# Products with kv and key sums as two matmuls of 64 stationary columns each, and second-layer weight loads placed by due time alone

## The chip, the cores and the metric

The kernel runs on one core of a Trainium2 chip. The metric is the device time of one execution in microseconds (us); less is better. TensorE (PE in the profile) multiplies matrices: it loads a stationary operand of up to 128 columns (PEld, the weight load), streams a moving operand past it and adds into PSUM. VectorE (DVE) and ScalarE (ACT) do everything elementwise, SyncE (SP) issues the DMAs. Each engine works through its own queue in order and waits for the others by semaphores. TensorE's clock is granted at one of two levels, 1.2 or 2.4 GHz; the profile gives it as a share of the upper one.

## The reference, cut to what matters

Linear attention with random features, then two feed-forward layers on its output:

```python
def phi(x):
    proj = np.einsum('bhsd,md->bhsm', x, omega)
    h = proj - np.sum(x * x, axis=-1, keepdims=True) / 2.0
    h = h - np.max(h, axis=-1, keepdims=True)
    return np.exp(h) / np.sqrt(m)
q_p, k_p = phi(q * scale), phi(k * scale)
kv = np.einsum('bhsm,bhsd->bhmd', k_p, v)           # key sums, 128 features x 64 per head
z = np.sum(k_p, axis=2)
num = np.einsum('bhsm,bhmd->bhsd', q_p, kv)         # products with kv
den = np.einsum('bhsm,bhm->bhs', q_p, z)[..., None] + 1e-06
x = (num / den)                                     # 4 batches x 576 tokens, 8 heads x 64
...
h = x @ w_in;  x = softplus(h) @ w_out              # layer 1: 512 -> 2048 -> 512
h = x @ w_in2; x = silu(h) @ w_out2                 # layer 2, the same sizes
```

There are 4 batches, 8 heads, 576 tokens a batch, 64 elements a head and 128 features. The layers' weights come as float64 and are turned into pairs of float32 parts on the core.

## The kernel before

**The attention.** The tokens are cut into 8 tiles of 256 (two a batch, n = 0 to 7) and one tile of the 256 tokens that are left (n = 8, 64 of each batch). `k_half` handles four heads of a key tile: two projections (`pp_k`), row maxima on DVE, the exponential on ACT (`phi`), and then the key sums `pkv_k` at L489: for each of the two pairs of heads (e = 0, 1) four products of float32, stationary operand a 128x128 tile of phi, moving operand 64 columns of v and a column of ones, so 65. The result is added to the batch's sums `kv` on DVE. `q_half` does the same for queries, and then transposes phi on TensorE (`pq`, L541), copies it back on ACT (`qt`, L545), multiplies it with `kv` (`pn`, L553: again four products of 128 stationary and 65 moving columns for each e), divides by the last column on DVE (`den`, `xn`, L564 to L567), and transposes the quotient on TensorE (`px`, L575), from which ACT and DVE make the layer's input `x`. A product of float32 shows as two passes in the trace, each a weight load and a matmul. The query tile n = 8 mixes four batches; its products at L557 already have 64 stationary columns, two beside each other: one for the first 64 tokens of the tile, written to PSUM partitions 0 to 63, the other for the second 64 tokens, to partitions 64 to 127.

**The layers.** The 2304 tokens go through as five blocks (sb = 0 to 3 of 512, sb = 4 of 256). In a block each of 16 chunks (fc) of the 2048 inner columns takes 12 matmuls `h` (L633 to L635; three products of high and low parts for each of four slices), then ACT and DVE make `g` and its two parts `ghl`, then 12 matmuls `y` (L656 in layer 1, L664 in layer 2). I write H(layer, sb, fc) and Y(layer, sb, fc) for these groups of 12. The attention of batch b + 1 runs between the groups of block (0, b); the attention of batch 0 comes ahead of all.

**Weights.** `weights(layer, fc, io, after)` loads 512 KB of float64 (`raw`, L278) and makes the two float32 parts from them: on ACT L284 and L301, on DVE L288, L292, L296 and the difference at L209. A raw tile sits in one of 4 buffers of tag `b4`, the finished weights in one of 16 of tag `wt`. The second layer's weights take over the buffers of the first layer's, and are made during block (0, 4) and block (1, 0).

**What sets the order.** Nothing of this is ordered by hand. Every step is given to `Order` (L53) with its engine, a planned cost, what it depends on, the buffers that it takes, and a due time. `due1` (L247 to L254) holds the planned time at which each H starts; steps get due times by counting back from it. `run` (L93) then simulates four engines and takes, for the engine that can start earliest, the step with the least due time among those that could start within 0.05 us of each other. `after` is the earliest planned time of a load. So each number in the cost table (L41 to L50) and each `after` can move any instruction on any engine. The layers' weights, `x`, and the attention share DVE, ACT and SP.

Of the kernel before, what the change touches and what calls it, by code (L numbers as in the profile page):

```python
# [28 lines left out]
NT = NB - 1  # L29
# [8 lines left out]

G1, G2, G3 = 0.2267, 0.117, 0.224  # L41
V5, V2, VS = (0.60, 0.15), (0.33, 0.15), (0.15, 0.15)
VF, VA, VH = (0.33, 0.15), (0.20, 0.15), (0.35, 0.15)
A5, A2, AE, AL, AX2 = (0.52, 0.17), (0.30, 0.15), (1.0, 0.2), (0.97, 0.17), (1.02, 0.2)
# [146 lines left out]
def attention_moe_moe_kernel(  # L191
# [15 lines left out]
    def diff(o, a, b):  # L207

        nc.vector.tensor_tensor(o, a, b, op=ALU.subtract)  # L209

    E = mybir.EngineType
    ctx.enter_context(tc.manual_schedule(engines={E.SP, E.Activation, E.DVE, E.PE}))
    const = ctx.enter_context(tc.tile_pool(name="const", bufs=1))
# [34 lines left out]
    for layer in range(2):  # L248
        for sb in range(NSB):
            full = width[sb] == 2 * T  # L250
            for fc in range(NFC):
                due1[layer, sb, fc] = t
                t += (24 * G1 if full else 12 * (G2 + (G1 / 2 if layer else G2))) + ((1.9 if sb else 2.2) if layer == 0 and sb < B else 0)
    due1["end"] = t  # L254

    def bits_pair():
# [214 lines left out]
    def k_half(n, half, simple, psums, due, after):  # L471
        s = {}
        name = f"k{n}_{half}"
        hs = slice(4 * half, 4 * half + 4)
        ins = inputs(s, name, kT[n, :, 2 * half : 2 * half + 2, :], kN[n, :, :, hs, :], [(v1[n, :, :, hs, :], (2, 4))], simple, simple, after)
        cols, sq_of = main_cols()
        phis = features(s, name, simple, ins, cols, sq_of, psums)
        tk = new(psums())
        b, h0 = n // 2, 4 * half
        both = []  # L480
        for e, (x, tphi) in enumerate(phis):

            def kv(e=e):
                phi, v = s["phi", e], s["v", 0]
                if "pkv" not in s:
                    s["pkv"] = get(tk["tag"], [P, 4, D + 1], F32, f"pkv_{name}")
                for j in range(2):
                    for c in range(2):
                        nc.tensor.matmul(  # L489
                            s["pkv"][:, 2 * e + j], phi[:, 2 * c + j, :], v[:, c, 2 * e + j, :], start=(c == 0), stop=(c == 1)  # L490
                        )

            both.append(add("PE", 4 * G3, kv, [x, ins[4][0]] + both, alloc=[] if e else [tk], uses=[tphi, ins[5][0]] + ([tk] if e else [])))
        chain(b, h0, add("DVE", VH, lambda: kv_add(b, h0, s["pkv"]), both, due=due, uses=[tk]))

    def k_tail(bp, simple, psums, due, after):
# [25 lines left out]
    def q_half(n, half, simple, psums, due, after):  # L522
# [12 lines left out]
        for e, (x, tphi) in enumerate(phis):  # L535
# [11 lines left out]
            def num(e=e, tn=tn):  # L547
                pn = s["pn", e] = get(tn["tag"], [P, 4, D + 1], F32, f"pn_{name}_{e}")
                qt = s["qt", e]
                for i in range(4):  # L550
                    h = 4 * half + 2 * e + i % 2
                    if n < NT:
                        nc.tensor.matmul(pn[:, i, :], qt[:, i, :], kvs[n // 2][:, h, :], start=True, stop=True)  # L553
                    else:
                        for a in range(2):
                            rs = slice(a * TAIL, (a + 1) * TAIL)
                            nc.tensor.matmul(  # L557
                                pn[rs, i, :], qt[:, i, rs], kvs[2 * (i // 2) + a][:, h, :], start=True, stop=True
                            )
# [23 lines left out]
                sums = [i for b in range(B) for i in kv_last[b, half]]  # L583
            f1 = add("PE", 0.45, flip, [x], alloc=[tq], uses=[tphi])
            c1 = add("ACT", A5, copy, [f1], alloc=[tqs], uses=[tq])
            n1 = add("PE", (4 if n < NT else 8) * G3, num, [c1] + sums, alloc=[tn], uses=[tqs])
            o1 = add("DVE", (0.5, 0.2), norm, [n1], alloc=[td, txn], uses=[tn])
            backs.append(add("PE", 0.23, back, [o1] + backs, alloc=[] if e else [tx], uses=[txn] + ([tx] if e else [])))

# [184 lines left out]
    for sb in range(NSB):  # L774
        if sb + 1 < NSB:
            attention(sb + 1, late_banks)
        if sb == NSB - 1:
            for fc in range(NFC):
                for io in range(2):
                    weights(1, fc, io, due1[0, NSB - 1, 0] + 2.8 * fc + 2.0)  # L780
        block(0, sb)
    for sb in range(NSB):
        x2(sb, due1[1, sb, 0] - 25.0)
# [66 lines left out]
```

## Time and profile before

| what | value |
|---|---|
| three runs, median | 972.95 us (972.69 to 976.61) |
| the profiled execution | 972.0 us, of it 970.2 us span from the first to the last instruction |
| PE matmuls | 943.5 us busy, 97% of the span, 4936 passes |
| PE weight loads | 803.3 us busy, 83% |
| DVE | 427.6 us busy, 44% |
| ACT | 443.3 us busy, 46% |
| mean granted TensorE clock | 0.994 |
| L553, `pn` with 128 stationary columns | 256 passes, 31.2 us busy, mean 275 ns |
| L489, `pkv` | 128 passes with v in `x_k` (16.2 us) and 128 with v in `v_k` (16.0 us) |
| L557, `pn` with 64 stationary columns | 64 passes, 2.3 us busy |

How to read it: matmuls are pipelined, so the busy time of a row of matmuls is the union of overlapping spans, and the duration of one (275 ns) is its way through the array, not the time that it keeps the next one waiting. What a matmul costs in a stream is the distance from its start to the next one's. Shares over the whole span hide that DVE and ACT are nearly full in the first fifth and mostly idle later.

### The profile page before, as it was taken

Reading aid. Unit: us, or ns where it says so; the run is one execution under the profiler, and the core shown is the slowest. Engines: PE = TensorE matmul, PEld = TensorE weight load, DVE = VectorE, ACT = ScalarE, POOL = GpSimd, SP = SyncE. Lnnn points to the kernel's source line nnn. Section 1 sums busy time; section 2 is a strip of 40 time slices with the busy share of each in tenths; the row PEclk is TensorE's granted clock in tenths of the full one; section 3 lists DMA queues with packets and bytes.
Section 4 is the critical chain, followed back from the end, with each engine's and each line's share of the span. In section 5 each row is a group of like instructions: output and inputs, shape, how many; then the busy total and the mean of one; then the engine's idle time right before and its main releaser. Section 6 shows DMA issues by size and latency. Waiting matters only on the chain.

```text
span 970.2 us, 12523 instructions
## 1 busy us (share of the span) xinstructions
PE 943.5 (97%) x4936; PEld 803.3 (83%) x4936; DVE 427.6 (44%) x923; ACT 443.3 (46%) x810; POOL 1.2 (0%) x7
## 2 busy tenths in 40 slices
PE   8899999999999999999999999999999999999994
PEld 7678778888888888887889988888888888888893
DVE  6987889455535453442112999521111112111210
ACT  7888878555555555442213776332222122221220
POOL 0000000000000000000000000000000000000000
PEclk9999999999999999999999999999999999999998
DMA  9643443222012221010003666202002000100100
GB/s 332 217 141 131 154 151 109 87 88 77 22 34 77 78 65 33 1 45 1 0 1 131 217 197 217 75 12 76 0 9 79 1 1 11 60 1 6 44 1 22
DMA packets 38159, 72.86 MB, mean 75 GB/s; under 512 B 3412, under 2 KB 18388, under 8 KB 38100
## 3 DMA queue, kind: packets, MB, share of 16 engines
q1 hardware_dynamic: 37970, 71.79, 22.0%
q8 instruction: 39, 0.64, 0.3%
q10 hardware_dynamic: 130, 0.26, 0.1%
q14 instruction: 20, 0.16, 0.1%
HBM read 62.60 MB, written 9.44 MB: 74 GB/s over the span
## 4 chain that ended last, share of the span: by engine, by line
PE 86%; DVE 5%; ACT 5%; DMA 2%; issue 1%; SPq 0%; ACTq 0%; DVEq 0%
PE y L664 20%; PE y L656 18%; PE h L633 13%; PE h L635 13%; PE h L634 13%; PE pkv_k L489 2%; PE pn_q L553 2%; PE pq_q L541 1%; DMA xN_q<-in_qN 1%; ACT phi_k L429 1%; DVE wt L209 1%; DVE wf L292 1%; ACT L641 1%; ACT L429 1%; PE px_q L575 1%
## 5 line engine op out<-in xcount | busy, mean ns | idle before, releaser
L209 DVE TENSOR_TENSOR ghl<-g,ghl 128x512 fp32r<-128x512 f32 (+1 forms) x160 | 101.9, 637 | 413.1 <-ACT ghl L642 411.6
L641 ACT ACTIVATE g<-h 128x512 f32<-128x512 f32 (+1 forms) x160 | 88.6, 554 | 333.4 <-PE h L635 332.9
L633 PE MATMUL h<-x,wt 128*128 128x512 f32 (+1 forms) x640 | 238.2, 372 | 0.4 <-ACT ghl L642 0.4
L634 PE MATMUL h<-x,wt 128*128 128x512 f32 (+1 forms) x640 | 235.8, 368 | 0.9 <-DVE x L209 0.9
L635 PE MATMUL h<-x,wt 128*128 128x512 f32 (+1 forms) x640 | 236.0, 369 | 0.0
L656 PE MATMUL y<-ghl,wt 128*128 128x512 f32 (+1 forms) x960 | 213.8, 372 | 0.0
L664 PE MATMUL y<-wt,ghl 128*128 128x512 f32 x864 | 208.6, 390 | 0.0
L656 PEld LDWEIGHTS y<-ghl,wt 128*128 128x128 f32 x960 | 166.2, 189 | 28.4
L664 PEld LDWEIGHTS y<-wt,ghl 128*128 128x128 f32 x864 | 161.3, 188 | 32.8
L634 PEld LDWEIGHTS h<-x,wt 128*128 128x128 f32 x640 | 120.8, 189 | 21.0 <-DVE x L209 1.3
L633 PEld LDWEIGHTS h<-x,wt 128*128 128x128 f32 x640 | 120.7, 189 | 20.4 <-ACT ghl L642 0.8
L635 PEld LDWEIGHTS h<-x,wt 128*128 128x128 f32 x640 | 120.7, 189 | 20.4
L642 ACT ACTIVATE ghl<-h 128x512 fp32r<-128x512 f32 (+1 forms) x160 | 88.1, 550 | 35.7 <-PE y L664 29.3
L284 ACT ACTIVATE wf<-raw 128x512 f32<-128x512 f32 x64 | 43.1, 681 | 13.8 <-DVE wt L209 13.5
L301 ACT CAST wt<-wf 128x512 fp32r<-128x512 f32 x64 | 39.4, 624 | 16.4 <-DVE wf L296 15.9
L209 DVE TENSOR_TENSOR wt<-wf,wt 128x512 fp32r<-128x512 f32 x64 | 43.2, 685 | 5.3 <-ACT wt L301 5.2
L292 DVE SCALAR_TENSOR_TENSOR wf<-wf,raw 128x512 uint32<-128x512 uint32 x64 | 43.0, 685 | 1.5 <-ACT wf L284 1.1
L296 DVE SCALAR_TENSOR_TENSOR wf<-raw,wf 128x512 uint32<-128x512 uint32 x64 | 43.1, 684 | 0.2
L641 ACT ACT_TABLE_LOAD x29 | 37.2, 1283 | 11.8 <-PE h L635 11.5
L409 DVE TENSOR_REDUCE mn_q<-pp_q 128x4 f32<-128x512 f32 x36 | 24.4, 686 | 24.3 <-PE pp_q L405 24.3
L553 PEld LDWEIGHTS pn_q<-kv,qt_q 128*128 128x128 f32 x256 | 30.8, 192 | 5.0 <-ACT qt_q L545 4.1
L553 PE MATMUL pn_q<-kv,qt_q 128*128 128x65 f32 x256 | 31.2, 275 | 2.4 <-ACT qt_q L545 2.4
(103 smaller groups left out, 708.8 us busy)
## 6 DMA issues: line engine op xcount, KB each, us to landing
raw<-in_w SPq DMA_DIRECT2D x64, 512.0 KB, 3.7
out<-y_sb SPq DMA_DIRECT2D x17, 256.0 KB, 2.2
y_dram<-y_sb SPq DMA_DIRECT2D x16, 256.0 KB, 2.0
x2raw<-y_dram SPq DMA_DIRECT2D x16, 256.0 KB, 3.8
xT_q<-in_qT SPq DMA_DIRECT2D x14, 256.0 KB, 2.9
xN_q<-in_qN SPq DMA_DIRECT2D x14, 256.0 KB, 3.1
x_k<-in_v SPq DMA_DIRECT2D x8, 260.0 KB, 5.3
v_k<-in_v SPq DMA_DIRECT2D x8, 260.0 KB, 3.0
```

The costliest lines, as they stand in the source:

```text
L209: nc.vector.tensor_tensor(o, a, b, op=ALU.subtract)
L284: nc.scalar.activation(s["f"], hif, AF.Copy, scale=2.0**-112)
L292: nc.vector.scalar_tensor_tensor(fu, fu, 3, lo, op0=ALU.logical_shift_left, op1=ALU.bitwise_or)
L296: nc.vector.scalar_tensor_tensor(fu, hi, 0x80000000, fu, op0=ALU.bitwise_and, op1=ALU.bitwise_or)
L553: nc.tensor.matmul(pn[:, i, :], qt[:, i, :], kvs[n // 2][:, h, :], start=True, stop=True)
L633: nc.tensor.matmul(ph[:, :w], wt[:, 0, 0, cs], xt[:, 0, cc, :w], start=(cc == 0), stop=False)
L634: nc.tensor.matmul(ph[:, :w], wt[:, 0, 0, cs], xt[:, 1, cc, :w], start=False, stop=False)
L635: nc.tensor.matmul(ph[:, :w], wt[:, 0, 1, cs], xt[:, 0, cc, :w], start=False, stop=(cc == NCC - 1))
L641: nc.scalar.activation(g, s["h"][:, :w], f)
L642: nc.scalar.activation(ghl[:, 0, :w], s["h"][:, :w], f)
L656: nc.tensor.matmul(py[dm][:, :w], wt[:, 1, a, cs], g[:, x, :w], start=(first and i == 0), stop=(last and i == 2),)
L664: nc.tensor.matmul(py[c], g[:, x, cs], wt[:, 1, a, :], start=(first and i == 0), stop=(last and i == 2),)
```

## The change

- `by_halves` replaces each product of `pkv` and of `pn` for n < 8 by two matmuls: columns 0 to 63 of the stationary operand into PSUM partitions 0 to 63, columns 64 to 127 into partitions 64 to 127, both with the same 65 moving columns. There are 128 such products in `pkv` (16 `k_half`, 8 each) and 128 in `pn` (16 `q_half`, 8 each). The tail of the keys (L511) and everything else keep their shapes.
- The planner is told 0.116 us for such a product in place of 0.224 us (G4 for G3), and the same for the products of n = 8 at L557, whose planned total falls from 8 * 0.224 to 4 * 0.116 us for each e.
- The planned allowance for attention in each chunk of blocks (0, 1) to (0, 3) falls from 1.9 to 1.6 us.
- The loads of the second layer's weights lose their earliest planned time.

```diff
-G1, G2, G3 = 0.2267, 0.117, 0.224
+G1, G2, G3, G4 = 0.2267, 0.117, 0.224, 0.116
...
+    def by_halves(o, a, b, **flags):
+
+        for c in range(2):
+            r = slice(c * 64, c * 64 + 64)
+            nc.tensor.matmul(o[r], a[:, r], b, **flags)
...
-                t += (24 * G1 if full else 12 * (G2 + (G1 / 2 if layer else G2))) + ((1.9 if sb else 2.2) if layer == 0 and sb < B else 0)
+                t += (24 * G1 if full else 12 * (G2 + (G1 / 2 if layer else G2))) + ((1.6 if sb else 2.2) if layer == 0 and sb < B else 0)
...
-                        nc.tensor.matmul(
-                            s["pkv"][:, 2 * e + j], phi[:, 2 * c + j, :], v[:, c, 2 * e + j, :], start=(c == 0), stop=(c == 1)
-                        )
-
-            both.append(add("PE", 4 * G3, kv, [x, ins[4][0]] + both, alloc=[] if e else [tk], uses=[tphi, ins[5][0]] + ([tk] if e else [])))
+                        by_halves(s["pkv"][:, 2 * e + j], phi[:, 2 * c + j, :], v[:, c, 2 * e + j, :], start=(c == 0), stop=(c == 1))
+
+            both.append(add("PE", 4 * G4, kv, [x, ins[4][0]] + both, alloc=[] if e else [tk], uses=[tphi, ins[5][0]] + ([tk] if e else [])))
...
-                        nc.tensor.matmul(pn[:, i, :], qt[:, i, :], kvs[n // 2][:, h, :], start=True, stop=True)
+                        by_halves(pn[:, i, :], qt[:, i, :], kvs[n // 2][:, h, :], start=True, stop=True)
...
-            n1 = add("PE", (4 if n < NT else 8) * G3, num, [c1] + sums, alloc=[tn], uses=[tqs])
+            n1 = add("PE", 4 * G4, num, [c1] + sums, alloc=[tn], uses=[tqs])
...
-                    weights(1, fc, io, due1[0, NSB - 1, 0] + 2.8 * fc + 2.0)
+                    weights(1, fc, io, 0.0)
```

Because the planner's numbers change, the order changes nearly everywhere in small ways. `pkv` still stands in runs of four products, each between other matmuls, and `pn` in runs of eight (e = 0 and 1 behind each other). Three places are shown as the built programs have them.

The first is on PE, in block (0, 3): the end of the second half of the query tile n = 8, whose quotient DVE makes before `px` can transpose it. Before:

```order
L557 MATMUL pn_q8_1_1_4179<-kv2_90,qt_q8_1_1_4163 64x65
L557 MATMUL pn_q8_1_1_4179<-kv3_91,qt_q8_1_1_4163 64x65
L575 MATMUL px_q8_1_4193<-ident_74,xn_q8_1_0_4191 128x128 x2
L656 MATMUL y_0_3_0_4049<-ghl_0_3_3_4134,wt_0_3_723 128x512 x3
L656 MATMUL y_0_3_1_4050<-ghl_0_3_3_4134,wt_0_3_723 128x512 x3
L656 MATMUL y_0_3_2_4051<-ghl_0_3_3_4134,wt_0_3_723 128x512 x3
L656 MATMUL y_0_3_3_4052<-ghl_0_3_3_4134,wt_0_3_723 128x512 x3
L575 MATMUL px_q8_1_4193<-ident_74,xn_q8_1_1_4211 128x128 x2
```

and now:

```order
L561 MATMUL pn_q8_1_1_4458<-kv2_90,qt_q8_1_1_4445 64x65
L561 MATMUL pn_q8_1_1_4458<-kv3_91,qt_q8_1_1_4445 64x65
L660 MATMUL y_0_3_0_4353<-ghl_0_3_3_4386,wt_0_3_830 128x512 x3
L660 MATMUL y_0_3_1_4354<-ghl_0_3_3_4386,wt_0_3_830 128x512 x3
L660 MATMUL y_0_3_2_4355<-ghl_0_3_3_4386,wt_0_3_830 128x512 x3
L660 MATMUL y_0_3_3_4356<-ghl_0_3_3_4386,wt_0_3_830 128x512 x3
L579 MATMUL px_q8_1_4491<-ident_74,xn_q8_1_0_4470 128x128 x2
```

The first `px` stood right behind the products and now stands behind the 12 matmuls of Y(0, 3, 3). For the first half of the tile (q8_0) the same happens with H(0, 3, 2).

The second is on PE at the end of block (0, 1), at the last query half of batch 2, q5_1. Before:

```order
L553 MATMUL pn_q5_1_0_2858<-kv2_90,qt_q5_1_0_2839 128x65 x4
L553 MATMUL pn_q5_1_1_2867<-kv2_90,qt_q5_1_1_2856 128x65 x4
L656 MATMUL y_0_1_0_1971<-ghl_0_1_14_2824,wt_0_14_1693 128x512 x3
L656 MATMUL y_0_1_1_1972<-ghl_0_1_14_2824,wt_0_14_1693 128x512 x3
L656 MATMUL y_0_1_2_1973<-ghl_0_1_14_2824,wt_0_14_1693 128x512 x3
L656 MATMUL y_0_1_3_1974<-ghl_0_1_14_2824,wt_0_14_1693 128x512 x3
L575 MATMUL px_q5_1_2895<-ident_74,xn_q5_1_0_2875 128x128 x2
```

and now:

```order
L660 MATMUL y_0_1_0_2106<-ghl_0_1_15_3038,wt_0_15_1910 128x512 x3
L660 MATMUL y_0_1_1_2107<-ghl_0_1_15_3038,wt_0_15_1910 128x512 x3
L660 MATMUL y_0_1_2_2108<-ghl_0_1_15_3038,wt_0_15_1910 128x512 x3
L660 MATMUL y_0_1_3_2109<-ghl_0_1_15_3038,wt_0_15_1910 128x512 x3
L215 MATMUL pn_q5_1_0_3071<-kv2_90,qt_q5_1_0_3053 64x65 x8
L215 MATMUL pn_q5_1_1_3080<-kv2_90,qt_q5_1_1_3069 64x65 x8
L579 MATMUL px_q5_1_3099<-ident_74,xn_q5_1_0_3092 128x128 x2
```

Here `px` moved the other way, to right behind the products that feed it. The same is so in block (0, 0) for q2_1 and q3_0, and there `pn` of q3_1 now follows its transposes `pq` with nothing between them.

The third is on SP, in block (0, 4): the loads of the second layer's weights (raw_1_fc_io) and of its first input (x2raw_0). Before:

```order
L278 DMA raw_1_2_1_4872<-in_w2 128x512
L278 DMA raw_1_4_0_4896<-in_w2 128x512
L278 DMA raw_1_3_1_4952<-in_w2 128x512
L719 DMA x2raw_0_0_4955<-y_dram_73 128x512
L719 DMA x2raw_0_1_4973<-y_dram_73 128x512
L719 DMA x2raw_0_2_4980<-y_dram_73 128x512
L278 DMA raw_1_5_0_4985<-in_w2 128x512
L278 DMA raw_1_4_1_5025<-in_w2 128x512
L278 DMA raw_1_6_0_5042<-in_w2 128x512
L719 DMA x2raw_0_3_5047<-y_dram_73 128x512
```

and now:

```order
L284 DMA raw_1_5_1_5232<-in_w2 128x512
L284 DMA raw_1_7_0_5236<-in_w2 128x512
L284 DMA raw_1_6_1_5294<-in_w2 128x512
L284 DMA raw_1_8_0_5318<-in_w2 128x512
L723 DMA x2raw_0_0_5372<-y_dram_73 128x512
L723 DMA x2raw_0_1_5376<-y_dram_73 128x512
L723 DMA x2raw_0_2_5395<-y_dram_73 128x512
L284 DMA raw_1_7_1_5401<-in_w2 128x512
L284 DMA raw_1_9_0_5406<-in_w2 128x512
L723 DMA x2raw_0_3_5447<-y_dram_73 128x512
```

Six of the weight loads now stand ahead of the stores of block (0, 3), and x2raw_0_0 stands behind 16 weight loads where it stood behind 9.

## Rows read from the trace of the kernel before

**Rows 1.** Busy time by stretch: PE, PEld, DVE, ACT, POOL busy (instructions), PEclk, DMA share, GB/s.

```profile
30.00:142.00 112.00, 104.55 (x562) 87.30 (x561) 93.39 (x222) 93.07 (x189) 0.00 (x0) 0.98 0.45 148
142.00:424.00 282.00, 282.00 (x1555) 243.56 (x1554) 148.26 (x344) 157.98 (x228) 0.00 (x0) 1.00 0.19 60
520.00:560.00 40.00, 40.00 (x335) 39.96 (x334) 28.40 (x56) 23.47 (x53) 0.00 (x0) 1.00 0.61 209
560.00:600.00 40.00, 40.00 (x189) 33.59 (x188) 38.73 (x72) 28.24 (x50) 0.00 (x0) 1.00 0.65 219
```

**Rows 2.** Chain that ended last, 100 to 145: start us, us, what.

```profile
114.99 5.11 DMA xN_q<-in_qN
...
130.85 5.65 DMA xN_q<-in_qN
...
141.21 2.00 PE pn_q L553 x16
```

**Rows 3.** Waits of PE after 142: engine line waited for, us in total, times, longest.

```profile
PE px_q L575 <- DVE den_q L564: 2.3, 2, 1.7
```

**Rows 4.** Passes of L553 and L489 after 142: duration ns min/median/max, first and last start.

```profile
L553 PE MATMUL pn_q<-kv,qt_q x155: 217/275/276, 141.8 to 407.2; 128*128 128x65 f32 x155
L489 PE MATMUL pkv_k<-v_k,phi_k x128: 217/275/276, 182.7 to 340.9; 128*128 128x65 f32 x128
```

**Rows 5.** Timeline of PE around one run of `pn`, 128 columns: start us, us, what.

```profile
237.85 1.89 PE L553 MATMUL pn_q<-kv,qt_q 128*128 128x65 f32 x16
239.55 0.47 PE L633 MATMUL h<-x,wt 128*128 128x512 f32 x1
239.87 0.40 PE L634 MATMUL h<-x,wt 128*128 128x512 f32 x1
```

**Rows 6.** Timeline around the second run of L557, 64 columns.

```profile
447.31 0.39 PE L634 MATMUL h<-x,wt 128*128 128x512 f32 x1
447.54 0.39 PE L635 MATMUL h<-x,wt 128*128 128x512 f32 x1
447.85 1.01 PEld L557 LDWEIGHTS pn_q<-kv,qt_q 128*64 128x64 f32 x32 [0.35 <-issue]
447.86 1.15 PE L557 MATMUL pn_q<-kv,qt_q 128*64 128x65 f32 x32
450.72 0.41 PE L575 MATMUL px_q<-ident,xn_q 128*128 128x128 f32 x2 [1.71 <-DVE den_q L564]
```

**Rows 7.** Timeline of PE around one run of `pkv`.

```profile
211.41 1.00 PE L489 MATMUL pkv_k<-v_k,phi_k 128*128 128x65 f32 x8
212.21 0.71 PE L656 MATMUL y<-ghl,wt 128*128 128x512 f32 x2
```

**Rows 8.** Passes of L557 over the whole span, as in rows 4.

```profile
L557 PEld LDWEIGHTS pn_q<-kv,qt_q x64: 132/138/142, 424.0 to 448.7; 128*64 128x64 f32 x64
L557 PE MATMUL pn_q<-kv,qt_q x64: 218/222/271, 424.0 to 448.8; 128*64 128x65 f32 x64
```

**Rows 9.** Timeline around the first run of L557.

```profile
424.01 1.16 PE L557 MATMUL pn_q<-kv,qt_q 128*64 128x65 f32 x32
425.72 0.41 PE L575 MATMUL px_q<-ident,xn_q 128*128 128x128 f32 x2 [0.56 <-DVE den_q L564]
```

**Rows 10.** DVE's timeline, then all engines', at the start of block (1, 0).

```profile
558.43 0.68 DVE L209 TENSOR_TENSOR x<-x2raw,x 128x512 fp32r<-128x512 f32 x1
...
559.00 0.88 PE L656 MATMUL y<-ghl,wt 128*128 128x256 f32 x6
...
559.72 0.40 PE L633 MATMUL h<-x,wt 128*128 128x512 f32 x1
```

**Rows 11.** Timeline of PE at 45, in batch 0's attention, and the clock there.

```profile
46.73 1.49 PE L575 MATMUL px_q<-ident,xn_q 128*128 128x128 f32 x4 [1.32 <-DVE xn_q L567]
...
48.00:50.00 2.00, 2.00 (x11) 1.78 (x10) 2.00 (x5) 1.20 (x3) 0.00 (x0) 0.50 0.00 0
```

**Rows 12.** Waits of PE from 60 to 165.

```profile
PE pn_q L553 <- ACT qt_q L545: 2.2, 2, 1.3
```

## The prediction

> **What bounds the kernel now.** I read the busy times by stretch first, since shares over the whole span mix stages. From 142 on PE is busy without a gap (282.00 of 282 us, 40.00 of 40), with DVE and ACT at little more than half up to 424; from 30 to 142 PE, DVE and ACT are all between 83 and 93% busy [rows 1]. Then the chain of work that ended last: around 112 to 141 it runs through DVE, ACT and two loads of xN_q, and only from 141.21 does it stay on PE, beginning with a run of pn [rows 2]. Then PE's own waits: after 142 there are two, 2.3 us together, both at px of the query tile n = 8 [rows 3]. So after 141 each us taken from PE comes off the end, and ahead of 141 the order on DVE, ACT and SP decides.
>
> **What there is to save on PE.** Products behind 141: 10 of the 16 runs of pn (155 passes recorded of 160, 16 a run) and 16 of the 32 runs of pkv (128 passes, 8 a run) [rows 4]. The other 6 and 16 lie ahead of it.
>
> One run of pn (8 products, 16 passes) takes from its first start, 237.85, to the next matmul's, 239.55, 1.70 us; and that next matmul is followed only after 0.32 us (239.55 to 239.87) where 0.23 is usual (447.31 to 447.54), so 0.09 belongs to the run as well: 1.79 us [rows 5, 6]. A run of pkv (4 products) takes 211.41 to 212.21, 0.80, with the same 0.09 0.89 us [rows 7]. That is 0.112 us for a pass in both.
>
> The new form stands in the trace already: L557 has the same operands, 128x64 stationary and 65 moving, two halves to neighbouring PSUM partitions. Its run is 16 half products of each e pair, 32 passes, as many as a run of pn will have. Its way in: the matmul ahead of it starts at 447.54, its own first at 447.86, so 0.32 where 0.23 is usual: 0.09 more [rows 6]. Inside, 32 passes take 1.15 us less the last one's 0.22, 0.93 from the first start to the last, 0.030 a pass [rows 6, 8]. Since one load alone takes 138 ns, loads of the two halves must run beside each other and over their matmuls. A run of pkv will have 16 passes: 15 * 0.030 = 0.45.
>
> What no row shows is the way out, x: the time from the last start of 64 columns to when matmuls of 128 columns run at their own pitch again. After both runs of L557 px waits for DVE. Below: x = 0.17, what the 128-column form shows (16 passes at 0.108 put the last start near 239.47, the next at 239.55, and 0.09). Above: 0.87, the whole gap after the first run (424.01 + 0.93 = 424.94 to 425.72, and 0.09), of which the profile puts 0.56 on DVE [rows 9]. I take 0.25, as an estimate: on the way in the load of 64 columns began at 447.85, 0.08 ahead of the modelled end of the matmul before it (447.54 + 0.39), where otherwise loads run ahead under earlier matmuls; if the way out waits likewise, the load begins 0.22 - 0.08 = 0.14 after the last start and its matmul 0.11 (a pass of 128 columns) later [rows 6, 8].
>
> The Trainium skill bears on this: "TensorEngine Tiling (Array Packing)", section Tiling Modes, says that a change of the tiling mode drains TensorE. The way in agrees (0.09 us); if a change cost nothing on the way out, the sum below would be 2.2 us better.
>
> A run of pn then saves 1.79 - 0.09 - 0.93 - x = 0.77 - x, a run of pkv 0.89 - 0.09 - 0.45 - x = 0.35 - x. Together 10 * (0.77 - x) + 16 * (0.35 - x) = 13.3 - 26x, at x = 0.25 **6.8 us**. Runs of pkv give 0.10 each: with four products the change of mode eats most of it. The shorter runs uncover nothing after 141: DVE has 148 and ACT 158 busy of 282 us [rows 1].
>
> **What moves after 141.** px of n = 8 goes behind 12 matmuls in both halves. Its gaps were 0.78 (424.94 to 425.72) and 1.93 (448.79 to 450.72) [rows 6, 9]; what stays is x - 0.09 = 0.16 each. DVE needs less than the 2.7 us (12 * 0.23) that H or Y now give it: in the first case px could start 0.78 behind the last product. Gain 0.62 + 1.77 = **2.4 us**. At q5_1 px goes the other way, to right behind its products: there the gap of the first case returns, 0.78 for 0.16, a loss of **0.6 us**; with DVE queued up it is at most the second case's, 1.8.
>
> **Layer 2's weights.** Six raw loads go ahead of the stores of block (0, 3) on SP; they wait only for raw buffers that two tiles' conversion frees. PE stands still nowhere between 520 and 600 [rows 1], so an earlier start has nothing to give: 0. It can take: x2raw_0 goes behind 16 raw loads instead of 9, and H(1, 0, 0) stands behind x2's last pass on DVE. That pass ended at 559.11, H began at 559.72 and needs this slice only nine matmuls later, 2.1 us [rows 10]. Now the pass stands seven DVE operations, some 4 us, behind the last ghl of block (0, 4), while four groups Y of 1.4 us (12 matmuls of 256 columns at 0.12, from six in 0.88) stand between H(0, 4, 15) and H(1, 0, 0), and the nine matmuls come on top: 7.8 us against about 5.6, with an estimated 1.6 for the passes of ghl itself ahead. Covered by some 2 us; if the conversion lags, up to 3 us are lost here. In layer 2 Y(k) now follows H(k + 1) instead of H(k + 2), 24 matmuls or 5.4 us behind its H, for two passes of ACT and one of DVE (0.68 at 512 columns) [rows 10].
>
> **Ahead of 141.** In block (0, 0) two runs of pn and eight of pkv would save 2 * 0.52 + 8 * 0.10 = 1.8 us on PE, but PE isn't what the chain rests on. Against it px of q2_1 and q3_0 stand right behind pn, and pn of q3_1 right behind pq: each a new gap of 0.6 us (DVE free, as in the first case above) to 1.3 (DVE full, as at 46.73) [rows 9, 11], so 1.8 to 3.9 together. SP loads xN_q of q2_1 and q3 two places or more earlier than before, which may end the two waits of 2.2 us for qt that hang on those loads [rows 2, 12]. A PE gap ahead of a run of px was followed by 1.2 GHz around 48 to 50 (granted 0.50) [rows 11]; each more such stretch of 2 us at half the clock costs 1 us. I take 0 for all this, with -3 and +3 as ends. Batch 0's attention, with 4 runs of pn and 8 of pkv, stays with DVE: 0.
>
> **The sum.** -6.8 - 2.4 + 0.6 = -8.6 us at x = 0.25; in general -(15.3 - 27x). The profiled execution took 972.0 us, which makes 963.4; the runs' median is 972.95, which makes 964.4. I forecast **964.0 us**.
>
> **The rivals.**
> 1. The way out is as cheap as between runs of 128 columns (x = 0.17), and the front gains: -10.7 and up to -3: 958.5 to 961.5. For it: nothing but that the way in costs only 0.09.
> 2. The front takes it back: DVE, ACT and the new gaps ahead of 141, or x2(0) late at 560, eat 3 to 8 us: 967 to 972. For it: three new short paths in a stretch where DVE is 83% busy; against: two waits of the same kind go.
> 3. Slower: the way out is long. The gain is gone at 15.3 - 27x = 0, x = 0.57, and from x = 0.75 on the kernel is slower by over 0.5%; at the upper end, 0.87, it is +8.2: 980. For it: after both runs of L557 PE did stand still longer than that. Against: DVE's den and xn end where px starts, which explains the gap in full.
> 4. The halves don't run beside each other in the new places, so the change doesn't do what it says: four passes of 0.057 (two passes of one half in the time of four of both) make 0.23 for a product where two of 0.112 stood, and 26 changes of mode at 0.09 + 0.08 make +4.4: about 975. Against: L557 has the same shapes and runs at 0.030 a pass [rows 6].
>
> Beside the fourth: "TensorE: Matmul & The Clock Gate" of the Trainium skill, Part 3, says that weight loads overlap matmuls in flight only when their row groups differ, and both halves use all 128 rows. By that rule the fourth would come true; L557's 32 loads of 138 ns in 1.01 us say otherwise.
>
> **How the numbers follow.** Forecast (961.5 to 967) 0.52, rival 1 0.15, rival 2 0.24, rivals 3 and 4 0.04 and 0.02, other losses 0.03. A measurement of this kernel tells about 0.5%, 4.9 us, from no change, so faster means under 968.1 and slower over 977.8. Forecast, rival 1 and a fifth of rival 2 are faster: 0.72; the rest of rival 2, rival 4 and part of the others 0.23; slower 0.05. The range that leaves out 2 in 10 goes from 959.5 (in rival 1) to 970.5 (in rival 2).
>
> **What would show it.** In the timeline of the changed kernel a run of pn should take 0.93 us for 32 passes and 1.18 from its first start to a steady stream, a run of pkv 0.45 and 0.70; the gap behind them gives x. PE's two waits at px of n = 8 should be gone, one of about 0.6 should stand at q5_1, and 520 to 600 should stay without a gap. H(0, 1, 0) should start where it did, within 3 us. The prediction is wrong if x is far from 0.25, or if the front moves by more than 3 us.

## The result and the profile after

Four runs of the changed kernel took 961.37 to 961.88 us, median 961.71; the kernel before beside it 972.82 (970.86 to 976.61). The ratio is 0.9881, with a 95% interval of 0.9851 to 0.9911: 11.1 us between the medians. The profiled executions differ by 10.2 us of span: 970.2 before, 960.0 after. One execution of the repeated runs below fell into a slow state (halves alone, 1169.47 us at a mean clock of 0.75) and is left out of its median.

Lines of `kernel.py` have moved: `by_halves` is L215 and makes `pkv` and `pn` for n < 8, `pn` of n = 8 is L561, `px` L579, `qt` L549, H is L637 to L639, Y L660. Busy time of the changed kernel by stretch (columns as in rows 1; the stretches are shifted by 8 or 10 us where the work is):

```profile
30.00:142.00 112.00, 100.72 (x739) 80.27 (x735) 93.76 (x225) 93.44 (x194) 0.00 (x0) 1.00 0.42 138
142.00:416.00 274.00, 272.97 (x1800) 226.58 (x1800) 148.26 (x340) 155.39 (x222) 0.00 (x0) 1.00 0.21 66
510.00:550.00 40.00, 40.00 (x336) 40.00 (x335) 34.82 (x67) 27.17 (x60) 0.00 (x0) 1.00 0.60 201
550.00:590.00 40.00, 40.00 (x188) 33.55 (x187) 38.84 (x73) 29.09 (x51) 0.00 (x0) 1.00 0.67 223
```

Behind 142 PE is as full as in [rows 1]: 1.03 us of 274 are idle. Its waits there, after 142 (engine line waited for: us in total, times, longest), against the 2.3 us at n = 8 in [rows 3]:

```profile
PE px_q L579 <- DVE den_q L568: 0.6, 1, 0.6
PE pn_q L215 <- ACT qt_q L549: 0.3, 1, 0.3
```

The first is the new one at q5_1. The two at n = 8 are gone: `px` now starts right behind the 12 matmuls that went ahead of it. PE's timeline around a run of `pkv`, the run of `pn` at q5_1, and both runs of n = 8 (start us, us, engine, line, what, idle time before it and what ended it):

```profile
210.43 0.69 PE L215 MATMUL pkv_k<-v_k,phi_k 128*64 128x65 f32 x16
211.04 0.50 PE L637 MATMUL h<-x,wt 128*128 128x512 f32 x1
211.38 0.39 PE L638 MATMUL h<-x,wt 128*128 128x512 f32 x1
...
292.70 1.15 PE L215 MATMUL pn_q<-kv,qt_q 128*64 128x65 f32 x32
294.41 0.41 PE L579 MATMUL px_q<-ident,xn_q 128*128 128x128 f32 x2 [0.56 <-DVE den_q L568]
...
418.85 1.16 PE L561 MATMUL pn_q<-kv,qt_q 128*64 128x65 f32 x32
419.93 0.50 PE L637 MATMUL h<-x,wt 128*128 128x512 f32 x1
420.27 0.39 PE L638 MATMUL h<-x,wt 128*128 128x512 f32 x1
...
439.31 1.15 PE L561 MATMUL pn_q<-kv,qt_q 128*64 128x65 f32 x32
440.39 3.04 PE L660 MATMUL y<-ghl,wt 128*128 128x512 f32 x12
443.26 0.38 PE L579 MATMUL px_q<-ident,xn_q 128*128 128x128 f32 x2
```

Here the way out can be read, which no row of before showed. A run of 32 passes takes 0.935 us from its first start to its last (1.15 less the last one's 0.22), so the next matmul (419.93) starts 0.15 behind the last start (418.85 + 0.935), and the one behind that after 0.34 where 0.23 is usual: x = 0.15 + 0.11 = 0.26. A run of `pn` with its weight loads (PEld) shows the parts:

```profile
239.48 1.02 PEld L215 LDWEIGHTS pn_q<-kv,qt_q 128*64 128x64 f32 x32 [0.35 <-issue]
239.48 1.15 PE L215 MATMUL pn_q<-kv,qt_q 128*64 128x65 f32 x32
240.56 0.19 PEld L637 LDWEIGHTS h<-x,wt 128*128 128x128 f32 x1
240.56 0.50 PE L637 MATMUL h<-x,wt 128*128 128x512 f32 x1
...
240.90 0.40 PE L638 MATMUL h<-x,wt 128*128 128x512 f32 x1
240.90 0.19 PEld L639 LDWEIGHTS h<-x,wt 128*128 128x128 f32 x1
...
241.14 0.39 PE L639 MATMUL h<-x,wt 128*128 128x512 f32 x1
```

The load of H begins 0.15 behind the last start of the halves, and the first matmul of H then takes 0.50 us where the next one takes 0.40.

For the rest I compare starts of the same piece of work, the first matmul of H(0, 0, 0), H(0, 0, 2), H(0, 1, 0), and the end of the span. Exactly as many matmuls of each kind lie ahead of H(0, 0, 2), and again ahead of H(0, 1, 0), in these four kernels, a product in halves counted as one; ahead of H(0, 0, 0) the new order has one run of `pkv` more (0.8 to 0.9 us). Each of the four was profiled twice (the second ones are the last experiments below); "half clock" is the time lost ahead of H(0, 1, 0) to a granted clock of 0.50 (1.2 GHz), summed over stretches of 2 or 4 us as their length times what the granted clock lacks to 1.00.

| kernel | half clock, where | H(0, 0, 0) | H(0, 0, 2) | H(0, 1, 0) | end of span |
|---|---|---|---|---|---|
| before | 1.7, at 46 to 50 | 53.95 | 68.37 | 177.24 | 970.2 |
| before, again | 3.4, at 140 to 150 | 53.66 | 68.07 | 180.70 | 973.6 |
| order alone | 3.4, at 48 to 56 | 58.11 | 69.93 | 178.62 | 969.9 |
| order alone, again | 5.1, at 46 to 58 | 57.25 | 69.03 | 177.75 | 969.0 |
| halves alone | 1.7, at 40 to 46 | 53.85 | 68.17 | 176.16 | 964.0 |
| halves alone, again | 3.4, at 46 to 56 | 56.11 | 69.82 | 177.52 | 965.3 |
| after | none | 54.74 | 66.38 | 173.86 | 960.0 |
| after, again | 1.7, at 44 to 50 | 54.63 | 66.29 | 173.81 | 959.9 |

The lines of H(0, 1, 0), before and after:

```profile
177.24 0.39 PE L633 MATMUL h<-x,wt 128*128 128x512 f32 x1
```

```profile
173.86 0.39 PE L637 MATMUL h<-x,wt 128*128 128x512 f32 x1
```

So of the 10.2 us, 6.8 were won behind H(0, 1, 0) and 3.4 ahead of it, where the sum had 1.0 (two runs of `pn` between 141 and 177). Of the 3.4, 2.0 stand at H(0, 0, 2) already. Behind H(0, 1, 0) the second profiles repeat the first within 0.1 us.

### The profile page after: what moved, and what is told of

Same layout as the page of the kernel before. It is cut to its first block, busy times and chain, and to the rows that moved or that the text cites. A ratio compares the mean times of both kernels' runs of the same rounds, so it can differ in the third digit from the quotient of the medians.

```text
span 960.0 us, 13554 instructions
## 1 busy us (share of the span) xinstructions
PE 930.4 (97%) x5448; PEld 776.4 (81%) x5448; DVE 428.0 (45%) x923; ACT 441.9 (46%) x810; POOL 1.2 (0%) x7
## 4 chain that ended last, share of the span: by engine, by line
PE 93%; DVE 4%; ACT 1%; DMA 1%; issue 0%; POOL 0%; DVEq 0%; ACTq 0%; POOLq 0%
PE y L660 21%; PE y L668 20%; PE h L637 14%; PE h L639 14%; PE h L638 14%; PE pkv_k L215 2%; PE pp_k L406 1%; PE pq_q L545 1%; PE pn_q L215 1%; PE pp_q L406 1%; PE px_q L579 1%; PE pp_k L409 1%; PE pp_q L409 1%; DMA raw<-in_w 1%; PE pp_q L411 0%; PE pp_q L410 0%
## 5 line engine op out<-in xcount | busy, mean ns | idle before, releaser
L637 PE MATMUL h<-x,wt 128*128 128x512 f32 (+1 forms) x640 | 238.3, 372 | 0.0
L639 PE MATMUL h<-x,wt 128*128 128x512 f32 (+1 forms) x640 | 236.0, 369 | 0.0
L660 PE MATMUL y<-ghl,wt 128*128 128x512 f32 (+1 forms) x960 | 213.2, 371 | 0.0
L660 PEld LDWEIGHTS y<-ghl,wt 128*128 128x128 f32 x960 | 166.0, 189 | 29.1
L639 PEld LDWEIGHTS h<-x,wt 128*128 128x128 f32 x640 | 120.6, 188 | 21.1 <-DVE wt L209 0.7
L637 PEld LDWEIGHTS h<-x,wt 128*128 128x128 f32 x640 | 120.7, 189 | 20.5
L290 ACT ACTIVATE wf<-raw 128x512 f32<-128x512 f32 x64 | 42.9, 686 | 12.8 <-DVE wt L209 12.2
L294 DVE TENSOR_SCALAR raw<-raw 128x512 uint32<-128x512 uint32 x64 | 26.3, 423 | 10.5 <-DMA raw<-in_w 10.4
L415 DVE TENSOR_REDUCE mn_k<-pp_k 128x4 f32<-128x512 f32 x32 | 22.0, 687 | 11.9 <-PE pp_k L411 7.7
```

Of the source, the lines that this page charges most:

```text
L290: nc.scalar.activation(s["f"], hif, AF.Copy, scale=2.0**-112)
L415: nc.vector.tensor_reduce(s["mn", e][:, :4], s["pp", e], op=ALU.max, axis=AX.X)
L637: nc.tensor.matmul(ph[:, :w], wt[:, 0, 0, cs], xt[:, 0, cc, :w], start=(cc == 0), stop=False)
L639: nc.tensor.matmul(ph[:, :w], wt[:, 0, 1, cs], xt[:, 0, cc, :w], start=False, stop=(cc == NCC - 1))
L660: nc.tensor.matmul(py[dm][:, :w], wt[:, 1, a, cs], g[:, x, :w], start=(first and i == 0), stop=(last and i == 2),)
```

## The experiments

**Order alone.** The planner's numbers and so the order are those of after, but each product is one matmul of 128 columns again.

```diff
     def by_halves(o, a, b, **flags):
-        for c in range(2):
-            r = slice(c * 64, c * 64 + 64)
-            nc.tensor.matmul(o[r], a[:, r], b, **flags)
+        nc.tensor.matmul(o, a, b, **flags)
```

> Every instruction stands where the changed kernel has it, on all engines, but each product with kv and each key sum is one matmul of 128 stationary columns again. Theory (halves and order both count, front gain from the shorter PE work): behind 177 us of the old trace it gains only the two px of n = 8 less the one of q5_1, 2.4 - 0.6 = 1.8 us, and nothing ahead: about 971 us. Rival (the 3.4 us that came off ahead of H(0, 1, 0) are the work of the new order on DVE, ACT and SP): 1.8 + 2.4 or more, 968 to 969 us. Runs of pn should be back at 1.79 us.

971.06 us (969.69 to 973.18), ratio 0.9977 (0.9962 to 0.9992). That is the theory's 971; the rival (968 to 969) falls, and runs of `pn` take 1.79 us again. The order by itself is worth 1 to 2 us. Its two places behind H(0, 1, 0) cost and give about what they were priced at: 2.3 us won at n = 8 (2.4 expected), 0.4 lost at q5_1 (0.6), and 0.2 lost in block (0, 2), which had no term: 1.7 together. Ahead of H(0, 1, 0) it loses 1.4 us.

**Halves alone.** The planner's numbers of before, so that PE, DVE, ACT and SP keep its order; the products in halves.

```diff
-...((1.6 if sb else 2.2) if layer == 0 and sb < B else 0)
+...((1.9 if sb else 2.2) if layer == 0 and sb < B else 0)
-            both.append(add("PE", 4 * G4, kv, ...
+            both.append(add("PE", 4 * G3, kv, ...
-            n1 = add("PE", 4 * G4, num, ...
+            n1 = add("PE", (4 if n < NT else 8) * G3, num, ...
-                    weights(1, fc, io, 0.0)
+                    weights(1, fc, io, due1[0, NSB - 1, 0] + 2.8 * fc + 2.0)
```

> The order of the kernel before on all engines, with halves in place of full products. Theory: behind 177 us 8 * 0.51 + 16 * 0.09 = 5.5 us less, the waits at px of n = 8 stay (0.78 and 1.93 long); ahead of 177 the two runs of pn on the chain give 1.0 and the rest of the front 0 to 2: 964.5 to 966.5 us. Rival (the order made the front's gain): exactly 6.5 us less, 966.4, with H(0, 1, 0) 1.0 us earlier than before. Rival (switching the array's mode costs more in other places): under 5 us less.

966.38 us (965.75 to 968.27), ratio 0.9922 (0.9892 to 0.9953). Behind H(0, 1, 0) the span gives 5.2 us, ahead of it 1.1. The theory (964.5 to 966.5) and the first rival (966.4) both allow that; what decides is the two runs together. Against the medians of before beside them (972.94) the parts make 1.9 + 6.6 = 8.5 us, the whole 11.1: some 2.6 us come only when both are there.

**The weights' part alone**, and **the change without it** (the due time of layer 2's weights back):

```diff
# the weights' part alone, against before
-                    weights(1, fc, io, due1[0, NSB - 1, 0] + 2.8 * fc + 2.0)
+                    weights(1, fc, io, 0.0)
# the change without it, against after
-                    weights(1, fc, io, 0.0)
+                    weights(1, fc, io, due1[0, NSB - 1, 0] + 2.8 * fc + 2.0)
```

> The kernel before with the second layer's weight loads by due time alone, and nothing else. Theory: PE has no gap between 520 and 600 that an earlier start could close, so no change: 972.8 within 0.7 us, with no PE wait at the start of block (1, 0). Rival: x2(0) comes late behind the weight loads, 1 to 3 us slower, seen as a PE wait at the first H of layer 2.

> The changed kernel with the second layer's weight loads held back by a planned time as before. Theory: that part is worth nothing: 961.7 within 0.7 us. Rival: it is worth what the change brought beyond the forecast, about 2 us: 963.5 to 964.

Alone: 970.81 us, ratio 0.9982 (0.9963 to 1.0001), no change that is clear of noise, and no wait at the start of layer 2. But it is 2 us under the 972.8 of the theory, and its profile shows where 1.2 of them lie (H(0, 1, 0) to the end 791.8 us, before 793.0): this part moved the order at n = 8 too, and the 2.3 us that PE waits there in [rows 3] became these:

```profile
PE px_q L575 <- DVE xn_q L567: 0.6, 1, 0.6
PE px_q L575 <- DVE den_q L564: 0.6, 1, 0.6
```

Without it: 963.79 us (962.71 to 964.99), 2 us over after, as the rival said; 1.6 of them lie behind H(0, 1, 0) in the profiles. Its trace has the place, with 1.0 us of waits. All its waits of PE behind 540, and PE and the transfer of x2 there:

```profile
PE h L637 <- ACT x L728: 0.8, 1, 0.8
PE h L638 <- DVE x L209: 0.2, 1, 0.2
```

```profile
543.22 1.38 SPq L723 DMA_DIRECT2D x2raw<-y_dram  x3
...
555.07 0.61 ACT L728 CAST x<-x2raw 128x512 fp32r<-128x512 f32 x1
555.71 0.69 DVE L209 TENSOR_TENSOR x<-x2raw,x 128x512 fp32r<-128x512 f32 x1
...
555.73 0.49 PE L637 MATMUL h<-x,wt 128*128 128x512 f32 x1 [0.78 <-ACT x L728]
```

and the same slices of x2 in the changed kernel:

```profile
540.26 1.37 SPq L723 DMA_DIRECT2D x2raw<-y_dram  x3
...
551.92 0.62 ACT L728 CAST x<-x2raw 128x512 fp32r<-128x512 f32 x1
552.82 0.68 DVE L209 TENSOR_TENSOR x<-x2raw,x 128x512 fp32r<-128x512 f32 x1
```

With the due time the first loads of x2 are issued 3.0 us later, and the last slice is cast at 555.07 instead of 551.92. That PE comes early is not the reason by itself: in halves alone, which has the due time too, H(1, 0, 0) starts at 553.45, only 0.7 us later than here (552.72), but the first loads of x2 were issued at 539.70 and the last cast began at 550.89, and PE doesn't wait. From the first load of x2 to H(1, 0, 0) it is 13.8 us there and in before, 9.5 here, 12.2 in after: the order that the planner's new numbers make together with the due time brings x2 late. The part is worth about 2 us with the rest, and about 1, in another place, without it.

**Only `pn` in halves**, in the order of after:

```diff
-                        by_halves(s["pkv"][:, 2 * e + j], phi[:, 2 * c + j, :], v[:, c, 2 * e + j, :], start=(c == 0), stop=(c == 1))
+                        nc.tensor.matmul(s["pkv"][:, 2 * e + j], phi[:, 2 * c + j, :], v[:, c, 2 * e + j, :], start=(c == 0), stop=(c == 1))
```

> The kernel after, with the key sums (pkv) back in one matmul of 128 stationary columns; the products pn stay in halves, and the order of every engine is that of after. Theory (a run of halves costs 0.26 us more at its way out, and saves 0.86 us inside a pn run and 0.44 inside a pkv run): the 16 pkv runs behind 141 us were worth 0.35 - 0.26 = 0.09 us each, 1.4 us in all, and the ones ahead of it at most as much again, so 963.1 to 964.5 us against 961.7 of after. Rival (short runs don't pay: one of four products gains less inside than its two changes of form cost): 961.0 to 961.7 us, no slower than after.

965.38 us (964.65 to 966.55), 0.9 over the top of the theory's range. From H(0, 1, 0) to the end it takes 787.4 us against 786.2 of after: 1.2 us for 16 runs, 0.08 each, as the theory has it (0.09). Ahead of H(0, 1, 0) it loses 1.5, of it 1.1 ahead of H(0, 0, 2), in a profile with 1.7 us of half clock. The rival falls: even runs of four products pay, though only just.

**The halves in series.** First the left columns of the four products, then the right ones:

```diff
-                for j in range(2):
-                    for c in range(2):
-                        by_halves(...)
+                for side in range(2):
+                    for j in range(2):
+                        for c in range(2):
+                            one_side(side, ...)
```

and the same for `pn`.

> The kernel after, but each run makes the first 64 columns of all of its four products and then the second 64 columns of all four, in place of the two halves of one product in turn; the same matmuls, the same order of steps. Theory (the 0.030 us a pass comes from two halves on different columns that load and run side by side): passes of one column half follow each other at about the 0.056 us of a full product, so a pn run takes about 1.8 us inside and a pkv run 0.9, as in full products, and the two changes of form come on top: 10 x 0.86 + 16 x 0.44 = 16 us behind 141 us, 976 to 980 us. Rival (a load of 64 columns is itself half as long, and no second half beside it is needed): 961.0 to 962.5 us, inner times unchanged at 0.93 and 0.46 us.

975.56 us (974.03 to 976.83): slower than before by 0.24% (0.09 to 0.39) with exactly the matmuls of after. A run of `pn` in it, on PE:

```profile
248.82 1.55 PE L214 MATMUL pn_q<-kv,qt_q 128*64 128x65 f32 x32
250.30 0.50 PE L639 MATMUL h<-x,wt 128*128 128x512 f32 x1
```

The rival falls: 32 passes take 1.33 us (1.55 less 0.22) instead of 0.935, and the 16 of `pkv` 0.75 instead of 0.46. The theory was right on the cause and wrong on the size: passes of one half do follow at 0.056 to 0.061 us within a group, but where one group of eight meets the next, which is of the other half, starts come in pairs, 0.003 to 0.006 us behind each other. I read that as groups that overlap at their ends; which half a start belongs to, the trace doesn't say. The run ends 0.4 us earlier than at 0.056 a pass throughout (31 * 0.056 = 1.74). What the order of a pair's halves is worth: 7.4 us behind H(0, 1, 0) (8 * 0.39 + 16 * 0.28 = 7.6 from the runs' own times), and 7.2 ahead of it, there together with 3.4 us of half clock.

The Trainium skill, "TensorE: Matmul & The Clock Gate", Part 3, has weight loads overlap matmuls in flight only when the row groups differ. The trace disagrees. Both halves use all 128 rows, and in after the 32 loads of a run of `pn`, 133 to 139 ns each, take 1.02 us together. Not even the columns have to differ: the load of 128 rows and 128 columns at 240.90 (0.19 us) lies under the matmul that started at 240.90, and the next one starts at 241.14. What two halves in turn add is the pace, 0.030 us a pass where passes of one half follow at 0.056 to 0.061.

**Key sums in runs of eight products.** From the third batch on the two steps e = 0 and e = 1 are one, which takes away eight of the 16 changes of form:

```diff
-            both.append(add("PE", 4 * G4, kv, ...
+            if simple:
+                both.append(add("PE", 4 * G4, kv, ...
+            elif e:
+                both.append(add("PE", 8 * G4, lambda: (kv(0), kv(1)), ...
```

> The kernel after, but from the third batch on the two key-sum steps of a chunk (four products each) are one step of eight products, so that eight runs of halves are saved with their ways in and out; nothing else of the products changes. Theory (way in 0.09 and way out 0.26 us are paid once a run whatever its length): 8 x 0.35 = 2.8 us at most where both steps were runs of their own, so 959.0 to 961 us. Rival (the longer step makes a waiting engine later, or the two steps already stood together): 961.2 to 963 us.

960.02 us (959.05 to 961.59), ratio to before 0.9860 (0.9836 to 0.9884): the fastest version here, though the runs of after, 961.37 to 963.72 in all, overlap with its own. Its profile has a span of 958.4, and from H(0, 1, 0) to the end it is 2.5 us shorter than after, where 2.8 was the most that eight changes of form at 0.35 could give.

**The query loads earlier.** Between 58 and 176 the chain of halves alone goes for 8.9% through loads of xN_q, that of after for a third through Y. So I gave these loads an earlier due time in halves alone:

```diff
-... nbytes=P * 2048, after=after)
+... nbytes=P * 2048, after=after, due=after + 40.0 - 22 if name[:2] in ("q2", "q3") else None)
```

> The halves alone in the order of before, with the loads of the third and fourth q chunk given an earlier due time on the DMA queue; PE's order is that of the halves alone (966.4 us, there 1.1 us ahead of before at the first H of batch 0's second chunk row, 177 us). Theory (between 58 and 141 us the late xN_q loads, 9% of the chain there, keep PE waiting, so shorter PE work gives nothing there; this is why halves and order together gave 3.6 us more than apart): the mark at 177 us comes 1.5 to 3 us earlier than in the halves alone, 963.5 to 965 us. Rival (DVE and ACT pace this stretch, and the load is only what the chain goes through): unchanged, 966.0 to 966.8 us.

965.95 us (963.88 to 966.73), and H(0, 1, 0) at 176.42 for 176.16: by these the rival holds. The pieces of the chain from 100 to 145 that took longest (start us, us, what), of halves alone and with the loads earlier:

```profile
...
114.89 5.08 DMA xN_q<-in_qN
130.72 5.47 DMA xN_q<-in_qN
```

```profile
102.61 1.28 ACT L435
104.43 1.66 ACT phi_q L435 x6
107.21 1.28 ACT L645
122.96 1.28 ACT L645
```

The loads are off the chain, and ACT and DVE take their place. But the run doesn't settle it, since only PE kept its order; the new due times moved steps on SP from 53 us on, on ACT and DVE from 76 and 84. PE's wait for `qt` ahead of the run of `pn` at 141 fell from 2.0 us (1.8 in the second profile of halves alone) to 0.3, and from H(0, 0, 2) to H(0, 1, 0) this kernel takes 106.0 us, halves alone 108.0 and 107.7: 1.7 to 2.0 less, which is what the theory wanted. H(0, 0, 2) itself came at 70.39, 2.2 and 0.6 us later than in halves alone, with 3.4 us of half clock ahead of it (1.7 and 3.4 there). So in that stretch the loads do cost PE time; whether the whole kernel gains by moving them is open.

**The four kernels once more**, unchanged, for second profiles and more times:

> The kernel after, unchanged, once more beside order alone, halves alone and before, so that the four can be compared at the same granted clock (the runs of before so far lie between 968.8 us of span at a mean clock of 0.994 and 975.0 at 0.988). Theory (2 to 3 us come only of order and halves together): at a mean clock of 0.993 or more the spans stand near 969.8 (before), 968.5 (order), 964.0 (halves) and 959.9 (after), so the whole of 9.9 is 2 to 3.5 us over the sum of its parts. Rival (that surplus was the half clock and the first loads of single executions): at equal clock the whole is within 1 us of the sum of the parts, after near 962 or halves near 962.

> Order alone, unchanged, once more. Both theories: a span of 968 to 969 us at a mean clock of 0.993 or more. In its profile the theory has the first H (54 to 58 us) 2 us or more behind that of after even where no half clock lies ahead of it; the rival has it within 1 us of that once the half clock is taken off.

> Before, unchanged, once more, for a second profile: the first H at 53.9 us and the one of the second chunk row at 177.2 us within 0.5 us if its clock loses 1.7 us ahead of them as in the first profile, and earlier by 0.7 us for each 0.96 us less of lost clock.

> Halves alone, unchanged, once more. Theory: span 964.0 at a mean clock of 0.993 or more, and the first H no earlier than before's by over 0.5 us although eight key-sum runs and four pn runs ahead of it are shorter, since waits take it back. Rival: the first H comes 2 us or more earlier than before's in an execution whose clock loses no more, and the span is near 962.

Medians 962.72, 971.60, 974.26 and 968.42 us. Among all executions with a mean clock of 0.993 or more the median spans are 969.8 (before, 23 executions), 967.9 (order, 3), 963.95 (halves, 2) and 959.9 (after, 6): 1.9 and 5.85 apart, 9.9 together. (The mean clock counts the end too: behind PE's last matmul it is 0.50 in each of these kernels' profiles, for 9 to 12 us, and costs PE nothing there.) The rival falls, but the surplus of 2.2 is at the low end of the theory, and two of the four medians rest on two or three executions. With the table above: halves give 1.1 us ahead of H(0, 1, 0) in the old order (first profiles; the second of before is disturbed at 140, below), in the new one 4.8 and 3.9.

The marks went less well. Order alone had 5.1 us of half clock ahead of H(0, 0, 0), so what it does without could not be seen. Halves alone put H(0, 0, 0) 2.2 us later than before's in its second profile, with 3.4 us of half clock ahead of it; its theory said only that it comes no earlier. And before, without half clock at 46 to 50, put H(0, 0, 0) only 0.3 us earlier, where 0.7 for each 0.96 of lost clock makes 1.2, and lost 3.4 us in another place. Its timeline there, and PE's busy time and clock (columns as in rows 1):

```profile
141.43 3.41 PE L553 MATMUL pn_q<-kv,qt_q 128*128 128x65 f32 x16 [1.81 <-ACT qt_q L545]
144.60 0.77 PE L633 MATMUL h<-x,wt 128*128 128x512 f32 x1
145.17 0.63 PE L634 MATMUL h<-x,wt 128*128 128x512 f32 x1
```

```profile
136.00:140.00 4.00, 3.62 (x21) 2.79 (x18) 3.08 (x7) 3.66 (x7) 0.00 (x0) 1.00 0.15 57
140.00:144.00 4.00, 2.57 (x14) 2.57 (x14) 2.65 (x6) 3.57 (x7) 0.00 (x0) 0.72 0.72 251
144.00:148.00 4.00, 4.00 (x12) 3.32 (x13) 3.06 (x9) 0.68 (x1) 0.00 (x0) 0.50 0.06 17
```

It is the run of `pn` at 141.21 of [rows 2]. In the first profile PE waited 1.33 us ahead of it and the clock stayed; here 1.81, and half the clock followed. The wait alone doesn't decide, for in halves alone PE waited 2.02 us at this place and the clock stayed at 1.00:

```profile
140.88 1.18 PE L215 MATMUL pn_q<-kv,qt_q 128*64 128x65 f32 x32 [2.02 <-ACT qt_q L549]
```

```profile
140.00:144.00 4.00, 3.12 (x41) 2.71 (x42) 2.69 (x9) 3.02 (x6) 0.00 (x0) 1.00 0.74 264
```

In both profiles of after the one wait for `qt` there is 0.3 us and the clock stands at 1.00.

## Why the prediction was right, point by point

- **The way out, x.** Estimated at 0.25, measured 0.26 behind every run that a matmul of H or Y follows, and made of what the estimate was made of: the load begins 0.15 behind the last start (0.14 estimated), and 0.11 more go before the stream has its pace. The way in (0.09) and the inside (0.93 and 0.46 us) are as read from the one place that already had the form. A run of `pn` saves 1.79 - 0.09 - 0.935 - 0.26 = 0.51 us, of `pkv` 0.89 - 0.09 - 0.46 - 0.26 = 0.08 (0.10 predicted). Rival 3 (a long way out) is out, and so is rival 4; the halves in series show what something like it would have cost.
- **The sum behind H(0, 1, 0).** 8 runs of `pn` and 16 of `pkv` lie there: 8 * 0.52 + 16 * 0.10 + 2.4 - 0.6 = 7.6 by the prediction's terms, 6.8 measured. Most of the 0.8 is in the halves: 5.1 (order alone to after) where the prediction's terms make 5.8 and the measured ones, 8 * 0.51 + 16 * 0.08, 5.4.
- **`px` at n = 8 and at q5_1.** 2.3 for 2.4. At q5_1 the loss is 0.4 with full products (order alone) and 0.6 in halves (block (0, 1) takes 122.45 us in after and 121.85 in halves alone), for 0.6. The gap at q5_1 is that of [rows 9] again: 0.56 us put on DVE there and 0.56 here.
- **Layer 2's weights.** "An earlier start has nothing to give: 0" failed. It was read from a PE that never waits in [rows 1], and so from the order of before. In the changed order the term is +2 us by the medians, 1.6 by the profiles; even in the order of before it was worth about 1, at n = 8, where no term stood. The loss feared for x2 came in the version without this part instead.
- **Ahead of 141.** Taken as 0 with ends at -3 and +3. H(0, 1, 0) came 3.4 us earlier, so one of the prediction's own signs of being wrong came true ("within 3 us"); with the 1.0 that was in the sum, 2.4 were not foreseen. The column H(0, 0, 2) tells where. From there to H(0, 1, 0) before takes 108.87 us, order alone 108.69 and 108.72, halves alone 107.99 and 107.70, after 107.48 and 107.52. The feared gaps show no net cost, and the halves give 0.9 to 1.2 in either order, about what the two runs of `pn` behind 141 are worth. So in block (0, 0) the term of 0 held, though Y makes 32.6% of the chain from 58 to 176 in after, 27.9% in order alone and 10.5% in before.
- **Batch 0's attention.** This is the term that failed: "stays with DVE: 0". In the order of before it did stay: 68.17 at H(0, 0, 2) in halves alone, 68.37 in before, both with 1.7 us of half clock. In the new order the halves bring H(0, 0, 2) from 69.93 and 69.03 to 66.38 and 66.29. Little of that is half clock: the change without the weights' part and the merged key sums have the order of after up to there and as much half clock as order alone in its first profile (3.4), and they stand at 66.82 and 67.53, 3.1 and 2.4 us ahead of its 69.93. The four runs of `pn` and eleven of `pkv` ahead of H(0, 0, 2) are worth 2.9.
- The 964.0 us are 2.3 over what was measured, inside the forecast's own range, by 0.2 us, but near rival 1, for that rival's second reason (the front) and not for its first (a cheap way out). That the total came so near is in part luck: 0.8 us too much behind H(0, 1, 0) and 2.4 too little ahead of it partly offset each other.

What stays open: why the new order lets the savings of batch 0's attention through and the old one doesn't. The surplus of 2 to 3 us stands at H(0, 0, 2) almost whole (3.4 of 3.7 by the first profiles), but no experiment moves single steps ahead of it; that it is the distribution of DVE's and ACT's work is only argued. How much of the 1.0 to 1.6 us that order alone loses up to there is its half clock can't be told: both of its profiles have it.

## What to carry to other kernels

A form that a kernel already uses in one place prices a change to it elsewhere: its way in, its inside and the order of its parts were there to read, and the one unknown could be put down to 0.01 us from how loads behave at the other edge. Price each run, not each instruction: a change of form is paid once a run, so a run of four products here gained 0.08 us and one of eight 0.51, and joining runs gained again. And a part that seems worth nothing in the old trace may be what the rest of the change needs: price it in the order that the whole change makes, not in the old one. Last, compare starts of the same work at several marks: by the chain from 58 to 176 the unforeseen gain looked like one of block (0, 0), by the marks most of it stands at H(0, 0, 2) already.

## What was not expected of the hardware

- Two column halves with the same rows start 0.007 us apart, pairs follow at 0.05 to 0.06 us, and the same passes ordered by halves take 1.33 us instead of 0.935.
- A granted clock of 0.50 did not cost what it lost. In after's second profile half the clock stands ahead of the first H, and H(0, 0, 0) came 0.1 us earlier than with 1.00 throughout, with PE idle 1.6 us less between 10 us and that mark (7.4 for 9.0) and DVE busy throughout in both. The same 2 us in after's first profile, then in the second:

```profile
46.00:48.00 2.00, 1.19 (x23) 0.95 (x21) 2.00 (x5) 1.96 (x4) 0.00 (x0) 1.00 0.44 156
```

```profile
46.00:48.00 2.00, 2.00 (x17) 1.62 (x18) 2.00 (x5) 1.89 (x4) 0.00 (x0) 0.50 0.52 170
```

- In before it fell now at 46 to 50, now at 140 to 150, and there cost all 3.4 us that it lost, while the 1.7 us at 46 to 50 cost 0.3 (H(0, 0, 0) at 53.95 and 53.66). Executions of before with a mean clock of 0.993 or more have a median span of 969.8 us, those with 0.991 or less 973.05; all eight executions of after lie within 959.6 and 961.8. So by this comparison some 1.2 of the 11.1 us between the medians (11.1 less the 9.9 at equal clock) go with clock that before loses and not with work saved.
